# Two expert layers after attention: the first layer's expert groups become four blocks wide, and its late weight conversions are spread over the steps

## The chip, the cores and the metric

The kernel runs on one core of a Trainium2 chip. The metric is the device time in microseconds (us), median of several runs; before the change it is 1189.27 us. The core has TensorE (PE in the profile; PEld is its weight load), VectorE (DVE), ScalarE (ACT), GpSimd (POOL) and SyncE (SP), which here only issues DMAs.

## The reference

```python
scores = scale * q @ k.T                       # (4, 8, 576, 576)
scores = where(scores >= max(scores) - tau, scores, -1e9)
attn   = exp(scores - max); attn /= sum(attn) + 1e-9
x = (attn @ v), heads side by side             # (2304, 512)
# layer 1, w_in (512, 2048), w_out (2048, 512), both float64 in memory
h = x @ w_in;  g = h * sigmoid(1.702 * h);  x = g @ w_out
# layer 2, its own w_in and w_out
h = x @ w_in;  g = max(0.01 * h, h);        out = g @ w_out
```

## The kernel before

**Attention.** The 32 heads are worked off in 16 pairs (`p` = 0 to 15). Each pair's operations have one- or two-letter names with a number (`Q8` are scores, `E8` the exponent, `w8`, `h8`, `l8` a copy and the two halves of flipped probabilities, `V` the products with the values, `a`, `b`, `c` what follows), and the table `START` gives each a time. The program is written out in the order of these times; an engine works through its own instructions in that order. In the last pair's table stand also some operations of layer 1: `Xh`, `Xl` (split of x), `H0`, `H1` (hidden sums) and `G21`, `G11`, `G20` (loads of weights).

**Number format.** TensorE multiplies rounded values. Each operand is a high half (rounded) and a low half (the rest), and each product is three products. So x of a block of 512 tokens becomes `xh` and `xl` (`split_x`: ACT copies, then POOL or DVE subtracts), and a weight block `wih`, `wil` or `woh`, `wol`.

**Weights.** `stage` (part G) loads one block of 128 columns of `w_in` (n = 0) or 128 rows of `w_out` (n = 1) as float64 into one of three buffers (`w64`); the SP queue issues the loads in program order, and a load waits until its buffer has been read. `convert` turns it into the two halves in parts: A on ACT (into the work tile `wF`), B, C, D, K on DVE, H on ACT (high half), M on POOL (low half). K is the last reader of the load's buffer.

**Expert layers.** `d_ff` is cut into 16 blocks `f`. The tokens are five blocks `blk`, four of 512 and the last of 256. A step is one (`blk`, `f`): `hidden_sums` (12 matmuls into `h`), the activation (ACT into `gf`, DVE multiplies or takes the maximum), the halves `gh` (ACT) and `gl` (POOL), and, LA = 2 steps later, `product` (12 matmuls into the four tiles `y`). `GROUPS` says how many `f` form a group. The steps go through group after group, in each through the token blocks, in each through the group's `f`. After the last `f` of a group in a block, `collect` adds `y` to x (or copies it, in the first group), and only then can the next block's product write the four tiles.

**Order.** While a group runs, the weights of the next are converted (`plan` puts each part of each block of weights into a step). Layer 1 had groups of 2, 4, 4, 4, 2, so two of its groups have ten steps; there the plan is `fast`, all parts of a block of weights in one step, between the DVE multiply of that step and its `gh`. Elsewhere it is `slow`, A to M over four steps. Three blocks of weights (`CONVERTED`) are converted in the first pair, three more (`STAGED`) are loaded ahead. `splits` splits the next block's x while a block runs.

Of the kernel before, what the change touches and what calls it, by code (L numbers as in the profile page):

```python
# [8 lines left out]
F32 = mybir.dt.float32  # L9
F32R = mybir.dt.float32r  # L10
I32 = mybir.dt.int32
AF = mybir.ActivationFunctionType
# [3 lines left out]
P = 128  # L16
B, H, S, D = 4, 8, 576, 64
NTOK = B * S
DM, DFF = 512, 2048
NCB = DM // P  # L20
NF = DFF // P
HALF = S // 2
NPAIR = B * H // 2
# [1 line left out]
SB = 3  # L25
TB = 512

GROUPS = {1: (2, 4, 4, 4, 2), 2: (4, 4, 4, 4)}
LA = 2
GB = 4  # L30
CONVERTED = ((0, 0), (1, 0), (0, 1))
STAGED = ((1, 1), (2, 0), (2, 1))
WI, WO = 8, 7
HI_MAX = 15 * 2.0**13 - 2.0**-7

# [133 lines left out]
    },  # L169
# [26 lines left out]
def split(a, n):  # L196
    return a.rearrange("p (h x) -> p h x", h=n)
# [3 lines left out]
def attention_moe_moe(  # L201
# [12 lines left out]
    nc = tc.nc  # L214
# [6 lines left out]
    stg = ctx.enter_context(tc.tile_pool(name="stg", bufs=1))  # L221
# [11 lines left out]
    tau_b = cp.tile([P, 1], F32, name="tau_b")  # L233
    tau_p = cp.tile([P, 1], F32, name="tau_p")
    qs = cp.tile([P, 1], F32, name="qs")

    wslot, staged, floats = {}, {}, {}
# [3 lines left out]
    def wtiles(layer, f, n):  # L241

        size, na = (WI, WO)[n], NA[n]
        early = ((layer - 1) * NF + f) % size < na
        return [
            pools["a" if early else "b"].tile(
                [P, DM], F32R, tag="w" + "io"[n] + z, name=f"w{'io'[n]}{z}_{layer}_{f}", bufs=na if early else size - na
            )
            for z in "hl"
        ]  # L250
# [13 lines left out]
    def convert(layer, f, n, part):  # L264
        src = staged[layer, f, n]
        if wide:

            words = src.rearrange("p (n t) -> p n t", t=2)
            lo, hi = words[:, :, 0], words[:, :, 1]
            if part == "A":  # L270
                floats[layer, f, n] = stg.tile([P, DM], F32, tag="wF", name=f"wF{layer}_{f}_{n}", bufs=2)
            F = floats[layer, f, n]
            t = F.bitcast(I32)
            if part == "A":
                nc.scalar.activation(F, hi.bitcast(F32), AF.Abs)
            elif part == "B":
                nc.vector.tensor_scalar(out=F, in0=F, scalar1=2.0**-15, scalar2=HI_MAX, op0=ALU.max, op1=ALU.min)  # L277
            elif part == "C":
                nc.vector.tensor_scalar(  # L279
                    out=t, in0=t, scalar1=3, scalar2=0x3FFFFFFF, op0=ALU.logical_shift_left, op1=ALU.bitwise_and  # L280
                )
            elif part == "D":
                nc.vector.scalar_tensor_tensor(
                    out=t, in0=lo, scalar=29, in1=t, op0=ALU.logical_shift_right, op1=ALU.bitwise_or
                )
            elif part == "K":
                nc.vector.scalar_tensor_tensor(  # L287
                    out=t, in0=hi, scalar=-0x40000000, in1=t, op0=ALU.bitwise_and, op1=ALU.bitwise_or
                )
        else:  # L290
            F = src
        if part == "H":
            wslot[layer, f, n] = wtiles(layer, f, n)
            nc.scalar.copy(wslot[layer, f, n][0], F)
        elif part == "M":
            wh, wl = wslot[layer, f, n]
            nc.gpsimd.tensor_tensor(out=wl, in0=F, in1=wh, op=ALU.subtract)
# [5 lines left out]
    def span(blk):  # L303
        return slice(blk * TB, min(NTOK, (blk + 1) * TB))

    def split_x(layer, blk, c, on, part=None):

        cols = span(blk)
        w = cols.stop - cols.start
        hs, ls = xs_of.setdefault((layer, blk), ({}, {}))  # L310
        for n, z in (("h", hs), ("l", ls)):
            if part not in (None, n):
                continue
            z[c] = pools["x0" if blk == 0 else "x"].tile(
                [P, w], F32R, tag=f"x{n}{c}_{blk}", name=f"x{n}{layer}_{blk}_{c}", bufs=1
            )
        if part != "l":
            nc.scalar.copy(hs[c], x[c][:, cols])  # L318
        if part != "h":
            on.tensor_tensor(out=ls[c], in0=x[c][:, cols], in1=hs[c], op=ALU.subtract)  # L320
# [19 lines left out]
    with tc.tile_pool(name="at", bufs=1) as at, tc.manual_schedule():  # L340
        qm = []
        for i in range(2):
            t = at.tile([P, 384], F32R, name=f"qm{i}")
# [122 lines left out]
        def exponent(p, t):  # L466
            r = st[p]
            e = at.tile([P, S], F32, tag="e", name=f"e{p}_{t}", bufs=2)
            nc.scalar.activation(  # L469
                split(e, 2), r["s", t][:, :, 0:HALF], AF.Exp, bias=r["m"][:, t : t + 1], scale=-1.0  # L470
            )
            r["e", t] = e

        def threshold(p, t):
            c = slice(t, t + 1)
# [298 lines left out]
        for f in range(NA[0]):  # L774
            LAST[f"H{f}"] = (lambda p, z: hidden_sums(1, 0, z), (f,))
        for f, n in STAGED:
            LAST[f"G{f}{n}"] = (lambda p, *z: stage(*z), (1, f, n))
# [7 lines left out]
        todo = []  # L785
# [74 lines left out]
    def collect(layer, blk, gi):  # L860
# [3 lines left out]
        for e, y in enumerate(y_of.pop((layer, blk))):  # L864
# [8 lines left out]
            if gi == 0:  # L873
                (nc.vector.tensor_copy if e % 2 else nc.scalar.copy)(acc, y)
            elif layer == 1 or gi < len(GROUPS[2]) - 1:
                nc.vector.tensor_tensor(out=acc, in0=y, in1=acc, op=ALU.add)  # L876
# [21 lines left out]
    steps, first_step, order = [], [], []  # L898
    for l in (1, 2):
        f0 = 0  # L900
        for gi, size in enumerate(GROUPS[l]):
            first_step.append(len(steps))
# [6 lines left out]
    todo = {}  # L909

    def plan(item, s, parts):
        for part, d in parts.items():
            todo.setdefault(max(0, s + d), []).append(item + (part,))

    slow = dict(G=-4, A=0, B=1, C=1, D=2, K=2, H=3, M=3)
    fast = dict(G=-2, A=0, B=0, C=0, D=0, K=0, H=0, M=0)
    for i, item in enumerate(z for z in order[0] if z[1:] not in CONVERTED):
        plan(item, i, fast)
    for g, items in enumerate(order[1:]):
        room = (first_step + [len(steps)])[g + 1] - first_step[g]  # L920
        for i, item in enumerate(items):
            if room < 2 * len(items) + 3:
                plan(item, first_step[g] + 1 + i, fast)
            else:
                plan(item, first_step[g] + 3 + 2 * i, slow)

    def weight_parts(s, which):
        for l, f, n, part in todo.get(s, ()):
            if part in which:
                if part != "G":  # L930
                    convert(l, f, n, part)
                elif (l, f, n) not in staged:
                    stage(l, f, n)

    def splits(s):

        l, gi, size, blk, f, j = steps[s]
        nxt = s - j + size
        if nxt >= len(steps) or steps[nxt][1] or (steps[nxt][0], steps[nxt][3]) == (1, 1):
            return  # L940
        for c in range(j * NCB // size, (j + 1) * NCB // size):
            split_x(steps[nxt][0], steps[nxt][3], c, nc.vector if size < NCB and c % 2 else nc.gpsimd)

    for c in range(NCB):
        split_x(1, 1, c, nc.vector if c % 2 else nc.gpsimd)
    for s in range(len(steps) + LA):
        weight_parts(s, "G")
        if s < len(steps):
            l, gi, size, blk, f, j = steps[s]
            rest = hidden(l, blk, f)  # L950
            weight_parts(s, "ABCDKH")
            rest()
            weight_parts(s, "M")
            splits(s)
        if s >= LA:
            l, gi, size, blk, f, j = steps[s - LA]
            product(l, blk, f, j == 0, j == size - 1)
            if j == size - 1:
                collect(l, blk, gi)
# [28 lines left out]
```

## Time and profile before

| | us |
|---|---|
| median of 3 runs (1187.96 to 1189.45) | 1189.27 |
| the profiled execution, its own time | 1188.86 |
| its span in the profile | 1187.1 |
| PE busy in the span | 1133.6 |
| DVE busy | 663.6 |
| ACT busy | 586.3 |
| POOL busy | 586.3 |

Busy time of PE is modelled from overlapping matmuls; idle stretches and the clock granted to TensorE tell more. The attention fills the first 352 us, layer 1 the time to about 791, layer 2 the rest.

### The profile page before, as it was taken

What the parts mean: (1) busy time and instruction counts of PE and PEld (TensorE: products, weight loads), DVE (VectorE), ACT (ScalarE), POOL (GpSimd) and SP (SyncE); (2) the same over time, 40 slices, a digit from 0 to 9 for tenths busy, and PEclk for the clock granted to TensorE, in tenths of its full rate; (3) what the DMA queues carried; (4) which work ended last, traced back from release to release, by engine and by line L of the source; (5) the groups of instructions that cost most, each with busy time, mean ns of one, the idle gap of its engine ahead of it and who ended that gap; (6) DMA issues with size and microseconds to landing.
All of it is one profiled execution on the core that took longest, in us unless ns stands there. A gap on an engine that the chain in (4) does not pass through costs nothing.

```text
span 1187.1 us, 17037 instructions
## 1 busy us (share of the span) xinstructions
PE 1133.6 (95%) x6201; PEld 968.2 (82%) x6201; DVE 663.6 (56%) x1357; ACT 586.3 (49%) x1138; POOL 586.3 (49%) x519
## 2 busy tenths in 40 slices
PE   8998999999896799999999999889999999999997
PEld 7887898889884588888888888778888888888886
DVE  6999999999876633443452524843343352534232
ACT  6998989999884432332332322334433332332221
POOL 6787887877774423343343332455543333343221
PEclk8999999999997989999999999999999999999999
DMA  5332323221302201110110100211110110110022
GB/s 145 82 84 64 82 61 98 70 72 35 103 1 72 70 19 36 54 54 18 54 54 18 54 18 19 90 35 37 53 54 18 54 54 18 54 36 1 36 63 62
DMA packets 47619, 62.38 MB, mean 53 GB/s; under 512 B 10544, under 2 KB 39216, under 8 KB 47536
## 3 DMA queue, kind: packets, MB, share of 16 engines
q1 hardware_dynamic: 47536, 61.29, 18.3%
q8 instruction: 49, 0.80, 0.3%
q14 instruction: 34, 0.28, 0.1%
HBM read 47.71 MB, written 4.72 MB: 44 GB/s over the span
## 4 chain that ended last, share of the span: by engine, by line
PE 69%; DVE 14%; ACT 10%; issue 3%; POOL 2%; DMA 1%; SPq 0%; DVEq 0%; ACTq 0%; POOLq 0%
PE h L332 30%; PE y L858 17%; PE y L856 13%; ACT e L469 3%; PE pv L585 3%; DVE m L462 3%; DVE pp L490 2%; PE s L435 2%; PE pp L511 2%; ACT raw L533 1%; DVE wF L277 1%; DVE wF L279 1%; DVE wF L287 1%; DVE x L876 1%; ACT ptg1h L542 1%
## 5 line engine op out<-in xcount | busy, mean ns | idle before, releaser
L828 POOL TENSOR_TENSOR gl<-gf,gh 128x512 fp32r<-128x512 f32 (+1 forms) x160 | 205.6, 1285 | 511.2 <-ACT gh L827 476.7
L824 DVE TENSOR_TENSOR gf<-h,gf 128x512 f32<-128x512 f32 (+1 forms) x80 | 51.0, 638 | 239.8 <-ACT gf L823 239.8
L332 PE MATMUL h<-xh,wih 128*128 128x512 f32 (+1 forms) x640 | 160.6, 371 | 17.5 <-ACT xh L318 17.5
L821 DVE TENSOR_TENSOR gf<-h,gf 128x512 f32<-128x512 f32 (+1 forms) x80 | 50.9, 637 | 207.6 <-ACT gf L820 207.6
L332 PE MATMUL h<-xl,wih 128*128 128x512 f32 (+1 forms) x640 | 160.8, 372 | 2.5 <-POOL xl L320 2.3
L823 ACT ACTIVATE gf<-h 128x512 f32<-128x512 f32 (+1 forms) x80 | 44.5, 556 | 233.8 <-PE h L332 230.7
L332 PE MATMUL h<-xh,wil 128*128 128x512 f32 (+1 forms) x640 | 159.2, 371 | 0.0
L332 PEld LDWEIGHTS h<-xh,wih 128*128 128x128 f32 x640 | 114.8, 188 | 41.7 <-ACT xh L318 20.5
L820 ACT ACTIVATE gf<-h 128x512 f32<-128x512 f32 (+1 forms) x80 | 44.4, 555 | 201.8 <-PE h L332 201.7
L332 PEld LDWEIGHTS h<-xl,wih 128*128 128x128 f32 x640 | 114.9, 191 | 25.0 <-POOL xl L320 5.0
L332 PEld LDWEIGHTS h<-xh,wil 128*128 128x128 f32 x640 | 114.7, 190 | 20.4
L856 PE MATMUL y<-gh,woh 128*128 128x512 f32 (+1 forms) x320 | 119.6, 378 | 8.1 <-DVE x L876 5.5
L827 ACT CAST gh<-gf 128x512 fp32r<-128x512 f32 (+1 forms) x160 | 92.5, 578 | 59.6 <-DVE gf L824 33.6
L856 PE MATMUL y<-gh,wol 128*128 128x512 f32 (+1 forms) x320 | 118.4, 374 | 0.0
L469 ACT ACTIVATE e<-s,m 128x576 f32<-128x576 f32 x144 | 110.8, 772 | 11.4 <-DVE m L462 10.2
L462 DVE TENSOR_REDUCE m<-s 128x1 f32<-128x576 f32 x144 | 107.7, 751 | 13.1 <-PE s L435 8.4
L858 PE MATMUL y<-woh,gh 128*128 128x512 f32 x288 | 112.4, 390 | 0.0
L858 PE MATMUL y<-wol,gh 128*128 128x512 f32 x288 | 112.3, 390 | 0.0
L435 PE MATMUL s<-kt,qt 128*128 128x288 f32 x512 | 100.3, 318 | 10.2 <-DVE pp L490 5.4
L490 DVE SCALAR_TENSOR_TENSOR pp<-s,thr,e 128x576 f32<-128x576 f32 x128 | 103.4, 810 | 7.9 <-ACT e L469 6.6
L856 PE MATMUL y<-gl,woh 128*128 128x512 f32 (+1 forms) x320 | 91.7, 371 | 0.0
L435 PEld LDWEIGHTS s<-kt,qt 128*128 128x128 f32 x512 | 73.2, 191 | 21.5 <-DVE pp L490 12.3
(117 smaller groups left out, 2209.0 us busy)
## 6 DMA issues: line engine op xcount, KB each, us to landing
w<-in_moe_w_in_dram SPq DMA_DIRECT2D x32, 512.0 KB, 3.6
w<-in_moe_w_out_dram SPq DMA_DIRECT2D x32, 512.0 KB, 3.6
kt<-kt SPq DMA_DIRECT2D x30, 288.0 KB, 4.1
kn<-in_k_dram SPq DMA_DIRECT2D x16, 256.0 KB, 2.9
qn<-in_q_dram SPq DMA_DIRECT2D x16, 256.0 KB, 2.9
vn<-in_v_dram SPq DMA_DIRECT2D x16, 256.0 KB, 3.0
out_dram<-o SPq DMA_DIRECT2D x20, 128.0 KB, 2.4
out_dram<-o SPq DMA_DIRECT2D x8, 256.0 KB, 2.2
```

The source lines that it names most:

```text
L332: nc.tensor.matmul(h, lhsT=wt[:, c * P : (c + 1) * P], rhs=xx[c], start=i == 0 and c == 0, stop=i == 2 and c == NCB - 1)
L435: nc.tensor.matmul(sc[:, a, 0:HALF], lhsT=w, rhs=kt[n][:, c : c + HALF], start=n == 0, stop=n == 1)
L462: nc.vector.tensor_reduce(out=small(p, "m")[:, t : t + 1], in_=r["s", t][:, :, 0:HALF], axis=mybir.AxisListType.XY, op=ALU.min)
L469: nc.scalar.activation(split(e, 2), r["s", t][:, :, 0:HALF], AF.Exp, bias=r["m"][:, t : t + 1], scale=-1.0)
L490: nc.vector.scalar_tensor_tensor(out=split(dst, 2), in0=r.pop(("s", t))[:, :, 0:HALF], scalar=r["thr"][:, t : t + 1], in1=split(r.pop(("e" ...
L821: nc.vector.tensor_tensor(out=gf, in0=h, in1=gf, op=ALU.mult)
L823: nc.scalar.activation(gf, h, AF.Copy, scale=0.01)
L824: nc.vector.tensor_tensor(out=gf, in0=h, in1=gf, op=ALU.max)
L827: nc.scalar.copy(gh, gf)
L828: nc.gpsimd.tensor_tensor(out=gl, in0=gf, in1=gh, op=ALU.subtract)
L856: nc.tensor.matmul(ys[e][:, 0:w], lhsT=wt[:, at_e], rhs=g, start=first, stop=last)
L858: nc.tensor.matmul(ys[e], lhsT=g[:, at_e], rhs=wt, start=first, stop=last)
```

## The change

- Layer 1's groups become four of four blocks, like layer 2's.
- The first group's own late weights (five blocks of weights after the three converted ones) are sorted by the step that needs them and spread: A two steps ahead, B, C, D, K one step ahead, H and M in the step itself; some of it stands ahead of the first step (`weight_parts(-1, ...)`). The loads ahead are now (2,0), (3,0) and (1,1).
- The second group's weights follow in the slow pattern, two steps apart.
- Within every step H now follows `gh`, M follows `gl`, and A comes after the splits; before, A and H stood ahead of `gh`.
- `wF` has three buffers in place of two.
- The split of layer 1's second token block, which stood ahead of the first step, is done one chunk a step in the first four steps, all on POOL.
- After the last exponent (`E8` of pair 15) a one-element-wide sigmoid is put on ACT.

```diff
-GROUPS = {1: (2, 4, 4, 4, 2), 2: (4, 4, 4, 4)}
+GROUPS = {1: (4, 4, 4, 4), 2: (4, 4, 4, 4)}
-STAGED = ((1, 1), (2, 0), (2, 1))
+STAGED = ((2, 0), (3, 0), (1, 1))
...
-        "G21": 214030, ... "G11": 344475, ... "G20": 388894,
+        "G11": 214030, ... "G20": 344475, ... "G30": 388894,
...
-                floats[layer, f, n] = stg.tile([P, DM], F32, tag="wF", name=f"wF{layer}_{f}_{n}", bufs=2)
+                floats[layer, f, n] = stg.tile([P, DM], F32, tag="wF", name=f"wF{layer}_{f}_{n}", bufs=3)
...
+            if (p, t) == (NPAIR - 1, 8):
+
+                nc.scalar.activation(tau_b, tau_p, AF.Sigmoid)
...
-            todo.setdefault(max(0, s + d), []).append(item + (part,))
-
-    slow = dict(G=-4, A=0, B=1, C=1, D=2, K=2, H=3, M=3)
-    fast = dict(G=-2, A=0, B=0, C=0, D=0, K=0, H=0, M=0)
-    for i, item in enumerate(z for z in order[0] if z[1:] not in CONVERTED):
-        plan(item, i, fast)
+            todo.setdefault(max(-1, s + d), []).append(item + (part,))
+
+    late = [z for z in order[0] if z[1:] not in CONVERTED]
+    late.sort(key=lambda z: z[1] + (LA if z[2] else 0))
+    for i, item in enumerate(late):
+        plan(item, i, dict(G=-4, A=-2, B=-1, C=-1, D=-1, K=-1, H=0, M=0))
     for g, items in enumerate(order[1:]):
-        room = (first_step + [len(steps)])[g + 1] - first_step[g]
         for i, item in enumerate(items):
-            if room < 2 * len(items) + 3:
-                plan(item, first_step[g] + 1 + i, fast)
-            else:
-                plan(item, first_step[g] + 3 + 2 * i, slow)
+            plan(item, first_step[g] + len(late) * (g == 0) + 3 * (g > 0) + 2 * i, dict(G=-4, A=0, B=1, C=1, D=2, K=2, H=3, M=3))
...
-        if nxt >= len(steps) or steps[nxt][1] or (steps[nxt][0], steps[nxt][3]) == (1, 1):
+        if nxt >= len(steps) or steps[nxt][1]:
...
-    for c in range(NCB):
-        split_x(1, 1, c, nc.vector if c % 2 else nc.gpsimd)
+    weight_parts(-1, "GABCDK")
     for s in range(len(steps) + LA):
         weight_parts(s, "G")
         if s < len(steps):
             l, gi, size, blk, f, j = steps[s]
             rest = hidden(l, blk, f)
-            weight_parts(s, "ABCDKH")
+            weight_parts(s, "BCDK")
             rest()
-            weight_parts(s, "M")
+            weight_parts(s, "HM")
             splits(s)
+            weight_parts(s, "A")
```

## Rows read from the trace of the kernel before

**Rows 1.** The page's 40 slices: granted clock of TensorE, in tenths.

```profile
PEclk8999999999997989999999999999999999999999
```

**Rows 2.** Stretches of the expert layers: busy time of each engine, granted clock, DMA.

```profile
352.04:426.78 74.74, 54.44 (x208) 41.88 (x205) 44.86 (x63) 33.02 (x63) 35.31 (x27) 0.84 0.21 64
728.65:794.26 65.61, 59.19 (x278) 47.22 (x277) 46.03 (x69) 24.36 (x45) 29.66 (x24) 1.00 0.21 65
```

**Rows 3.** The chain that ended last, in order of time: start, us, what.

```profile
417.97 4.79 PE y L856 x12
...
440.75 2.72 PE h L332 x12
...
511.46 1.43 PE h L332 x12
...
519.82 2.41 DVE x L876 x4
...
522.27 1.21 PE y L856 x8
```

**Rows 4.** TensorE in order of time; idle before an instruction in brackets.

```profile
352.04 1.20 PE L332 MATMUL h<-xh,wih 128*128 128x512 f32 x4
...
360.42 0.50 PE L856 MATMUL y<-gh,woh 128*128 128x512 f32 x1 [2.65 <-ACT gh L827]
```

**Rows 5.** Two stretches after idle TensorE, columns as in Rows 2.

```profile
379.74:384.50 4.76, 4.76 (x10) 3.28 (x11) 2.02 (x3) 1.44 (x3) 3.71 (x3) 0.50 0.21 77
384.90:393.00 8.10, 8.10 (x37) 6.70 (x36) 5.16 (x9) 4.32 (x8) 3.36 (x3) 1.00 0.21 65
```

**Rows 6.** TensorE in the second stretch of Rows 2.

```profile
771.82 0.47 PE L856 MATMUL y<-gh,woh 128*128 128x512 f32 x1 [1.86 <-DVE x L876]
```

**Rows 7.** ScalarE in order of time, end of the attention and first step.

```profile
344.42 0.74 ACT L469 ACTIVATE e<-s,m 128x576 f32<-128x576 f32 x1 [0.79 <-DVE m L462]
...
347.27 0.43 ACT L570 CAST rtg1h<-pr 128x320 fp32r<-128x320 f32 x1 [0.61 <-PE pr L556]
348.12 0.59 ACT L533 COPY raw<-pp 128x512 f32<-128x512 f32 x1 [0.43 <-PE pp L511]
...
350.20 0.21 ACT L619 ACTIVATE inv<-sum 128x5 f32<-128x5 f32 x1
...
352.10 2.18 ACT L318 CAST xh<-x 128x512 fp32r<-128x512 f32 x4
354.31 1.28 ACT L820 ACT_TABLE_LOAD   x1
```

**Rows 8.** Groups of instructions from 352 to 427 us, shapes apart: count, busy us, mean ns.

```profile
L828 POOL TENSOR_TENSOR gl<-gf,gh 128x512 fp32r<-128x512 f32 x8 | 10.3, 1287 | 31.7 <-ACT gh L827 31.7
...
L275 ACT ACTIVATE wF<-w 128x512 f32<-128x512 f32 x9 | 6.0, 662 | 0.0
...
L827 ACT CAST gh<-gf 128x512 fp32r<-128x512 f32 x8 | 4.9, 613 | 0.0
L820 ACT ACTIVATE gf<-h 128x512 f32<-128x512 f32 x8 | 4.8, 594 | 7.1 <-PE h L332 7.0
```

**Rows 9.** VectorE in order of time.

```profile
352.71 0.49 DVE L656 TENSOR_TENSOR x<-pn,xs 128x320 f32<-128x320 f32 x1
...
357.32 0.43 DVE L279 TENSOR_SCALAR wF<-wF 128x512 int32<-128x512 int32 x1
357.78 0.69 DVE L283 SCALAR_TENSOR_TENSOR wF<-w,wF 128x512 int32<-128x512 int32 x1
...
362.05 1.39 DVE L279 TENSOR_SCALAR wF<-wF 128x512 int32<-128x512 int32 x1
```

**Rows 10.** GpSimd in order of time.

```profile
361.69 1.46 POOL L297 TENSOR_TENSOR wol<-wF,woh 128x512 fp32r<-128x512 f32 x1
```

**Rows 11.** Loads of the weight buffers between 340 and 427 us.

```profile
DMA to landing us min/median/max: 3.5/3.6/3.8
```

**Rows 12.** TensorE in layer 2's first group.

```profile
870.18 0.39 PE L332 MATMUL h<-xl,wih 128*128 128x256 f32 x1 [0.60 <-POOL xl L320]
```

6 rows, old and new, of the table START are left out of this document.

## The prediction

> **What bounds the kernel now.** I read the 40 slices first: TensorE's granted clock is full but for three places, one of them around 355 to 425 us, where the attention hands over to layer 1 [rows 1]. The chain in order of time says what sets the end there: in steady state nothing but matmuls, 12 in 2.72 us for a full block and in 1.43 us for the half block [rows 3]. So a group of steps has a floor that can be counted, and a stretch's loss is its length less its matmuls.
>
> First group before, from H0's first matmul to the first hidden sum of group 2, 74.74 us [rows 2, 4]: 7 full and 2 half hidden sums and 8 full products, 15 x 2.72 + 2 x 1.43 = 43.7 us. Loss 31.1 us, at a granted clock of 0.84.
>
> Last group of layer 1 and the change to layer 2, 65.61 us [rows 2]: 10 full and 2 half hidden sums, 8 full and 3 half products, 18 x 2.72 + 5 x 1.43 = 56.1 us. Loss 9.5 us. One of its waits is 1.86 us of TensorE for an addition on VectorE, which stood behind four conversions in its queue [rows 6].
>
> These are the two groups of ten steps, planned `fast`. The groups of twenty lose little: at such a group's end the full product ends when VectorE's additions begin, 519.82; one half hidden sum (1.43) is all TensorE has before the next half product, whose last 8 matmuls begin at 522.27, behind those additions, and end at 523.48 [rows 3]. Without a wait that product would have ended at 519.82 + 2 x 1.43 = 522.68: 0.8 us an end.
>
> **The change part by part.** The matmuls stay the same. Three places change, and I walk each.
>
> *End of the attention.* The early sigmoid puts a table load of 1.28 us [rows 7] and a small activation (0.21, as the one of 128x5) behind E8, which ends at 345.16. ScalarE then has slack: 0.61 us before `rtg1h` and 0.43 before the last copy `raw` [rows 7]. So 1.5 - 1.04 = 0.5 to 0.6 us reach the attention's end. I take +0.6; below, 0, if more slack hides it; above, 1.5. The load that is removed (354.31) was no gain here: H0's matmuls, begun at 352.04, end only at about 354.8, so the first activation waits for them about as long [rows 4, 7]. The Trainium skill (ScalarE: Activation LUTs, What ACT_TABLE_LOAD costs) counts another 1.38 us of drain with each switch; the trace shows none, for the load begins where the casts before it end, 352.10 + 2.18 = 354.28 against 354.31 [rows 7]. By the page the sum below would be 1.4 us longer.
>
> *First group.* Five late blocks of weights are converted while the first steps run. What decides is how VectorE and GpSimd get along. Part C takes 0.43 us alone, but 1.39 when GpSimd runs beside it: it starts at 362.05, M ends at 361.69 + 1.46 = 363.15, C at 363.44 [rows 9, 10]. So one of the two waits for the other, and each gets in behind the other's current instruction. The parts cost, alone, B and C 0.45 each, D and K 0.72 with the gap [rows 9]; `gl` 1.29 [rows 8], and M and `xl`, of the same shape, as much. ScalarE: A 0.66, cast 0.61, `gf` 0.59 [rows 8]; the multiply as D, 0.7. In a step of the new plan stand B, C, D, K (2.3) and `gl`, M, `xl` (3.8): 6 us one after another, against 5.44 of matmuls. The walk, alternating, all 0.6 us later than before:
>
> - Ahead of the steps: VectorE is free at 353.20 + 0.6 = 353.8 [rows 9]; conversion of (2,0) to 356.1. H0 352.6 to 355.4.
> - Step 0: multiply to 356.8, `gh` 357.4, H of (2,0) 358.0. Then B, C of (1,1), `gl`, D, M of (2,0) (360.8), K (361.4), `xl` (362.7). Step 2's hidden sum starts at 358.0 and must wait at its fifth matmul for M; at 360.8 it goes on, at half clock 8 x 0.43, to 364.2. Product 0 to 366.9.
> - Step 1: the multiply waits for K, 361.4 to 362.1; `gh`, H, `xh` to 363.8. The load of (2,1) waited for K of (1,1) too: issued 361.5, landed 3.6 later [rows 11], 365.1. A of (2,1) stands in ScalarE's queue ahead of step 2's `gf`, which so starts at 365.8. VectorE and GpSimd alternate to K of (3,0), 368.2.
> - Step 2: multiply to 368.9, H of (3,0) 370.1, M 372.9. Hidden sum 3: four matmuls from 370.1 at half clock, the rest from 372.9 to 375.6. Product 1 to 378.3.
> - Step 3: `gf` 376.2, multiply 376.9, H of (2,1) 378.1, `gl` 379.0, M 380.9, last `xl` of block 1 382.8. Hidden sum 4 waits for it, to 383.0; product 2 385.7, hidden sum 5 388.5 (M of (3,1) is done by then, 387.5), product 3 391.2.
>
> From here TensorE has two steps' lead. Since 352.04 it has done 5 hidden sums and 4 products, 9 x 2.72 = 24.5 us, in 39.2: a loss of 14.7 us, the 0.6 included. Gain 31.1 - 14.7 = 16.4 us.
>
> The half clock: after 2.65 idle us [rows 4] and more, TensorE ran at a granted clock of 0.50, that is 1.2 of 2.4 GHz, for 4.8 us, then at 1.00 [rows 5]; 12 matmuls took 4.79 us in place of 2.72 [rows 3]. I have it twice in the walk; a third time, at product 2, would be +1.5.
>
> *Rest of group 1.* In the steps that follow the three engines fit into 5.44 us (GpSimd 2.6, every second step 3.9; VectorE 0.7 + 0.9 or 1.4). The chunk split in a block's last step is needed by the next hidden sum; layer 2's first group, built the same, lost 0.60 us by it [rows 12]: +0.6. The second group's conversions end two steps into it, ahead of their use. One more end of a twenty-step group (0 to 1): +0.8.
>
> *Layer 1 to layer 2.* The ten-step group goes; its place takes an end like the one above (0.8), with layer 2's first split in its four half steps: `gl` 0.7 (an estimate, a little over half of the full one's 1.29), `xl` 1.29, M 1.29 in two of four, conversions 0.9 or 1.4, some 15.2 us against 14.0 of matmuls. The last `xl` comes about 0.7 to 1.2 us late. Loss 2.0 in place of 9.5: gain 7.5; at best 8.7, at worst 4.
>
> A, H, M behind `gh`, `gl` in all other steps, and the third `wF` buffer: nothing; TensorE's work of two steps (10.9 us) hides them. Without that cover each would cost its 0.6.
>
> **Sum**, against the profiled execution: 1188.86 + 0.6 + 0.8 - 16.4 - 7.5 = 1166.4. The median shown is 0.4 above that execution, so **1167**.
>
> **The rivals.**
>
> *The engines do not block each other so much* (the lock rule is wrong in size, or `gl` and M fall between the conversions). The same walk with every instruction at its time alone ends the four products at 385.3, loss 8.8; with the best transition: 31.1 - 8.8 + 8.7 - 0.8 - 0.6 = 29.6 saved, 1159. For it: D and K at 0.69 in many places. Against: C at 1.39 [rows 9]. Chance 0.18.
>
> *The queue of ScalarE holds the group back.* (2,1) and (3,1) are not loaded ahead; the A that waits for the load stands ahead of the next `gf`, and that of everything else in the step; the clock falls a third time. Two late loads of some 2 us each beyond the walk, 1.5 of clock, and the transition at its worst: loss 20 and 5.5, saved 31.1 - 20 + 9.5 - 5.5 - 1.4 = 13.7, 1175. Chance 0.15.
>
> *Slower than before.* The walk has short waits in every one of the first steps. If these keep TensorE at the lower level on through the group, a full step costs 2 x 4.79 = 9.6 in place of 5.44 us; 22.5 / 4.2 = 5.4 such steps beyond the walk eat the gain, ten of them give 1209. Against it: once matmuls followed each other, the clock was back after 4.8 us [rows 5]. Chance 0.03.
>
> *The plan does not spread:* an in-order queue makes the first steps as serial as before, and only the last group's gain is left, within some us of 1181; chance 0.02. And 0.02 within 0.2%, which is about what a measurement of this kernel tells from no change.
>
> The Trainium skill (SBUF — State Buffer, SBUF: two separate sides) has a rule that speaks against putting this work side by side: VectorE in its two-port forms or with two SBUF inputs, and GpSimd, take one port pair by an exclusive lock, for a whole instruction. Rows 9 and 10 agree ([rows 9, 10]: C ends 0.29 us after M). By it the walk's 1167 holds, without it the first rival's 1159.
>
> **How the numbers follow.** Forecast 0.60, with its own range 1163 to 1171. The 8-in-10 range takes in the first rival's end and the second's: 1159 to 1175. Faster: 0.60 + 0.18 + 0.15 + 0.02 = 0.95; same 0.02; slower 0.03.
>
> **What would show it.** The sigmoid's table load behind E8 and H0 about 0.6 us later. B, C, D, K of (2,0) before the first multiply, about 353.8 to 356.1; C or D at some 1.3 us beside GpSimd in steps 0 to 3. Product 3 ends at about 391; from then on 5.44 us a step to the end of the block, no idle TensorE above 1 us before the group's end. Between layer 1 and 2 at most two waits, of about 1 us. The prediction is wrong if product 3 ends before 387 or after 396, if ScalarE waits for a load in every step, or if the transition still loses more than 5 us.

## The result, and the profile after

| | before | after | |
|---|---|---|---|
| median, us | 1188.77 (1187.96 to 1189.45, 4 runs) | 1169.22 (1168.12 to 1170.26, 4 runs) | ratio 0.9838, 95% interval 0.9823 to 0.9854 |
| profiled execution, its own time | 1188.86 | 1169.74 | 19.1 less |
| its span | 1187.1 | 1168.0 | 19.1 less |

One run of an experiment below, 1246.24 us at a granted clock of 0.845 where all others have 0.98 or more, is left out of its median. The forecast was 1167, its own range 1163 to 1171.

The 40 slices first, as in [rows 1]. Before, the granted clock was below 9 in the first slice, in the 13th (356 to 386 us, a 7) and in the 15th (415 to 445 us, an 8); the last two, which the prediction put down as one place, begin in the first group, and the change to layer 2 had no dip. After the change the 15th slice is at 9 and the 13th at 8.

```profile
PEclk8999999999998999999999999999999999999999
```

Then the stretches. The first row is the first group from H0's first matmul to the end of product 3; the next three are pieces of it; the last is the change from layer 1 to layer 2 (columns as in [rows 2]).

```profile
356.26:394.70 38.44, 30.00 (x113) 22.80 (x110) 22.98 (x24) 14.64 (x28) 22.56 (x16) 0.87 0.18 55
364.40:367.60 3.20, 3.20 (x8) 2.58 (x9) 3.17 (x4) 2.09 (x4) 3.01 (x3) 0.55 0.43 128
375.50:380.80 5.30, 5.29 (x13) 4.13 (x14) 1.28 (x3) 0.65 (x2) 1.64 (x1) 0.50 0.32 99
386.60:400.00 13.40, 13.40 (x61) 11.07 (x60) 4.13 (x7) 7.10 (x13) 6.61 (x6) 1.00 0.11 35
748.34:775.08 26.74, 25.98 (x157) 22.70 (x157) 12.29 (x23) 10.88 (x22) 19.04 (x16) 1.00 0.19 59
```

In the 38.44 us stand 5 hidden sums and 4 products, 24.5 us at the full rate: a loss of 14.0 us, where the walk had 14.1 behind H0. It has two stretches at half clock (0.55 and 0.50), as many as the walk counted, the second one four matmuls later than there; from 386.6 on TensorE is full. The change of layers holds 5 x 2.72 + 8 x 1.43 = 25.0 us of matmuls, so it loses 1.7 us (forecast 2.0; 9.5 before).

TensorE's waits in order of time, which answer to [rows 4, 6, 12]:

```profile
361.86 1.20 PE L332 MATMUL h<-xh,wih 128*128 128x512 f32 x4 [2.58 <-ACT wih L294]
364.38 2.08 PE L332 MATMUL h<-xh,wil 128*128 128x512 f32 x4 [1.32 <-POOL wil L297]
373.00 1.21 PE L332 MATMUL h<-xh,wih 128*128 128x512 f32 x4 [2.43 <-ACT wih L294]
375.51 2.07 PE L332 MATMUL h<-xh,wil 128*128 128x512 f32 x4 [1.30 <-POOL wil L297]
386.17 0.50 PE L332 MATMUL h<-xl,wih 128*128 128x512 f32 x1 [0.81 <-POOL xl L320]
451.78 0.39 PE L332 MATMUL h<-xl,wih 128*128 128x256 f32 x1 [0.60 <-POOL xl L320]
...
560.19 0.39 PE L859 MATMUL y<-gh,woh 128*128 128x256 f32 x1 [0.40 <-DVE x L879]
...
766.22 0.50 PE L332 MATMUL h<-xl,wih 128*128 128x512 f32 x1 [0.37 <-POOL xl L320]
```

The reader sees the walk here: hidden sum 2 waits for its high half, four matmuls later for its low half, and hidden sum 3 does the same. Counted from H0's first matmul, the walk had hidden sum 2 at 5.4 and 8.2 us (measured 5.6 and 8.1), hidden sum 3 at 17.5 and 20.3 (16.7 and 19.3), the last `xl` at 30.4 (29.9).

But H0 itself came at 356.26, in place of 352.04 [rows 4]: 4.2 us later, where the forecast had 0.6. The chain that ended last shows why (start, us, what):

```profile
318.11 6.14 DMA w<-in_moe_w_in_dram
324.27 0.69 ACT wF L275
324.98 0.44 DVE wF L277
325.44 0.44 DVE wF L279
325.90 0.69 DVE wF L283
...
328.00 0.60 DVE wF L287
...
348.57 1.28 ACT L475
349.86 0.20 ACT tau_b L475
```

Parts A to K of (2,0) run at 324 to 329 us, in the middle of the last pair of the attention, and not behind it at 353.8 as the walk had them. They need nothing of the attention, and they are written ahead of the steps; the built program has them before the last pair's own waiting work. So for these six instructions it does not hold that an engine works in the order in which the program is written out; what in the build moves them was not found out. ScalarE's row there waits for the load:

```profile
324.27 1.24 ACT L275 ACTIVATE wF<-w 128x512 f32<-128x512 f32 x2 [2.01 <-DMA w<-in_moe_w_in_dram]
...
348.57 1.28 ACT L475 ACT_TABLE_LOAD   x1
349.86 0.20 ACT L475 ACTIVATE tau_b<-tau_p 128x1 f32<-128x1 f32 x1
...
359.31 0.60 ACT L823 ACTIVATE gf<-h 128x512 f32<-128x512 f32 x1 [3.01 <-PE h L332]
...
362.23 0.66 ACT L275 ACTIVATE wF<-w 128x512 f32<-128x512 f32 x1
```

The 4.2 us split into three, by the first scores of the last pair behind its key exchange (321.20 before, 321.89 after), H1 (343.72, 347.11) and H0 (352.04, 356.26): 0.7 ahead of that pair, 22.52 to 25.22 = 2.7 in it, 8.32 to 9.15 = 0.8 from H1 to H0, where the early table load stands. The 0.7 need not be the change's: in the profiles of the changed kernel and of the edits below that lie behind that place, these first scores come anywhere from 320.02 to 322.75.

VectorE in the first steps, which answers to [rows 9]:

```profile
361.46 1.74 DVE L283 SCALAR_TENSOR_TENSOR wF<-w,wF 128x512 int32<-128x512 int32 x1
363.24 1.63 DVE L287 SCALAR_TENSOR_TENSOR wF<-w,wF 128x512 int32<-128x512 int32 x1
364.80 0.68 DVE L824 TENSOR_TENSOR gf<-h,gf 128x512 f32<-128x512 f32 x1
365.40 0.90 DVE L277 TENSOR_SCALAR wF<-wF 128x512 f32<-128x512 f32 x1
366.33 1.44 DVE L279 TENSOR_SCALAR wF<-wF 128x512 int32<-128x512 int32 x1
367.81 1.66 DVE L283 SCALAR_TENSOR_TENSOR wF<-w,wF 128x512 int32<-128x512 int32 x1
```

And GpSimd beside it, which answers to [rows 10]:

```profile
362.62 1.71 POOL L297 TENSOR_TENSOR wil<-wF,wih 128x512 fp32r<-128x512 f32 x1
364.29 1.73 POOL L320 TENSOR_TENSOR xl<-x,xh 128x512 fp32r<-128x512 f32 x1
366.20 1.28 POOL L831 TENSOR_TENSOR gl<-gf,gh 128x512 fp32r<-128x512 f32 x1 [0.19 <-ACT gh L830]
367.45 1.47 POOL L297 TENSOR_TENSOR wol<-wF,woh 128x512 fp32r<-128x512 f32 x1
```

Ends lie one behind the other: M to 364.33, K to 364.87, `xl` to 366.02, C to 367.77, M to 368.92, D to 369.47. Each engine gets in once between two instructions of the other, and D, 0.69 alone [rows 9], takes 1.66 and 1.74 here.

### The profile page after: what moved, and what is told of

It is laid out like the page before. It is cut to its first block, busy times and chain, and to the rows that moved or that the text cites. A ratio compares the mean times of both kernels' runs of the same rounds, so it can differ in the third digit from the quotient of the medians.

```text
span 1168.0 us, 16925 instructions
## 1 busy us (share of the span) xinstructions
PE 1129.2 (97%) x6201; PEld 968.5 (83%) x6201; DVE 639.3 (55%) x1327; ACT 589.1 (50%) x1139; POOL 602.6 (52%) x529
## 4 chain that ended last, share of the span: by engine, by line
PE 74%; DVE 10%; ACT 9%; issue 4%; POOL 2%; DMA 1%; DVEq 0%; ACTq 0%; SPq 0%; POOLq 0%
PE h L332 32%; PE y L861 17%; PE y L859 15%; ACT e L469 3%; DVE m L462 3%; PE pv L588 3%; DVE pp L493 2%; PE s L435 2%; PE pp L514 2%; ACT raw L536 1%; ACT ptg1h L545 1%; ACT kt L405 1%; ACT qt L413 1%; ACT sh L603 1%; POOL xl L320 1%
## 5 line engine op out<-in xcount | busy, mean ns | idle before, releaser
L831 POOL TENSOR_TENSOR gl<-gf,gh 128x512 fp32r<-128x512 f32 (+1 forms) x160 | 210.6, 1316 | 473.1 <-ACT gh L830 452.4
L332 PE MATMUL h<-xh,wih 128*128 128x512 f32 (+1 forms) x640 | 158.1, 369 | 5.0 <-ACT wih L294 5.0
L859 PE MATMUL y<-gl,woh 128*128 128x512 f32 (+1 forms) x320 | 88.5, 368 | 0.0
```

What stands on the lines that cost most here:

```text
L332: nc.tensor.matmul(h, lhsT=wt[:, c * P : (c + 1) * P], rhs=xx[c], start=i == 0 and c == 0, stop=i == 2 and c == NCB - 1)
L831: nc.gpsimd.tensor_tensor(out=gl, in0=gf, in1=gh, op=ALU.subtract)
L859: nc.tensor.matmul(ys[e][:, 0:w], lhsT=wt[:, at_e], rhs=g, start=first, stop=last)
```

## The experiments

Each kernel is the changed one with the edit shown; every ratio is to the kernel before, run beside it. "First group" is H0's first matmul to the end of product 3 (38.44 us in the changed kernel's profile), "last pair" the first scores behind the key exchange to H1 (25.22; 22.52 before). Behind product 3 all the changed kernels take the same time, 773.1 to 773.6 us to the end of the span, so what an edit is worth lies ahead of it. How often the clock falls in the first group differs from profile to profile (see the repeat at the end), which is worth 1.7 us there.

**The loads earlier.** The loads of (2,0) and (3,0) get earlier times in the last pair's table.

```diff
-        ... "G20": 344475, ... "G30": 388894, ...
+        ... "G20": 235000, "G30": 256000, ...
```

> The changed kernel with one edit: the three loads ahead, (1,1), (2,0), (3,0), are all issued before pair 14 instead of (2,0) and (3,0) in pair 15. Theory: the attention's end came 3.4 us later than before because ScalarE stood 2.0 us in pair 15, waiting for the load of (2,0) that the first conversion needs. Then the conversion finds its data, no such wait shows, H0 starts at about 353.5 to 354.5 instead of 356.3, and the time is 1.5 to 3 us below the changed kernel's 1169.2: 1166 to 1167.7. Rival: it is the conversion work itself (1.2 us of ScalarE, 2.2 us of VectorE) among the attention's instructions; then H0 starts where it did, within 0.7 us, and the time is that of the changed kernel within 0.7 us.

Measured: 1167.38 us (1166.69 to 1170.43), ratio 0.9827, 0.9808 to 0.9846. The last pair is back at 22.55 us, but the conversions moved with their load into the twelfth pair, and that pair went from some 16.1 to 19.08 us in the profiled execution (1170.43, the slowest of the four). ScalarE waits for no load there. H0 came at 357.06, 0.8 later than in the changed kernel, and not at 353.5 to 354.5. So in this profile work put into a pair costs about 3 us there as well; the other three runs (1166.7 to 1168.0) lie in the range of the theory and leave open whether it always does.

**The sigmoid table late.** The early one-element sigmoid is left out.

```diff
-            if (p, t) == (NPAIR - 1, 8):
-                nc.scalar.activation(tau_b, tau_p, AF.Sigmoid)
```

> The changed kernel without the small sigmoid behind the last exponent, so that the table is loaded ahead of the first activation of layer 1. Theory: ScalarE is idle for 3.0 us there, so the load of 1.28 us is hidden, and the attention's last copies come 0.8 us earlier: H0 at about 355.4 and the time 0.6 to 1.0 us below the changed kernel's. Rival: the load lies on the path at its new place; then the first activation comes up to 1.3 us later behind H0 and the time is the same or up to 0.5 us longer.

Measured: 1169.24 us (1168.95 to 1169.7), ratio 0.9838, 0.9823 to 0.9853. ScalarE in order of time:

```profile
355.63 1.28 ACT L820 ACT_TABLE_LOAD   x1
358.63 0.60 ACT L820 ACTIVATE gf<-h 128x512 f32<-128x512 f32 x1 [1.71 <-PE h L332]
```

The load is over at 356.91, and the activation still waits 1.71 us for H0's matmuls: it comes 3.06 us behind H0's first matmul (355.57) here and 3.05 in the changed kernel. From H1 to H0 it is 8.30 us in place of 9.15. So the early table costs 0.8 us at the attention's end and buys nothing; the expected gain of 0.6 to 1.0 us in the median did not show, and the medians do not resolve it.

**The old plan in the new groups.** The late weights have all parts in one step, and A and H stand ahead of `gh` again.

```diff
-        plan(item, i, dict(G=-4, A=-2, B=-1, C=-1, D=-1, K=-1, H=0, M=0))
+        plan(item, i, dict(G=-4, A=0, B=0, C=0, D=0, K=0, H=0, M=0))
...
-            weight_parts(s, "BCDK")
+            weight_parts(s, "ABCDKH")
             rest()
-            weight_parts(s, "HM")
+            weight_parts(s, "M")
             splits(s)
-            weight_parts(s, "A")
```

> The changed kernel with the late weights' conversions not spread: all parts A to H of one block of weights in one step, between the multiply and the high half of g, one block a step in steps 0 to 4, and A and H in that place in all later steps too; groups of four, sorted order, loads and table as in the changed kernel. Theory: most of the gain comes from the groups (the ten-step groups are gone), and the spreading is worth only the share of the first four steps: each step is a chain of A, B, C, D, K, H, cast, subtracts and a hidden sum, some 8 to 9 us, so product 3 ends 4 to 9 us later than in the changed kernel, less up to 3 us that the attention gains because no conversion stands in it: 1171 to 1176. Rival: the spreading brings most of it; then the time is above 1180.

Measured: 1175.43 us (1173.09 to 1175.85), ratio 0.9886, 0.987 to 0.9902. The first group, in the view of stretches:

```profile
353.56:400.94 47.38, 31.66 (x113) 23.06 (x109) 19.87 (x29) 16.78 (x31) 20.56 (x17) 0.86 0.18 56
```

The first group takes 8.9 us longer, the last pair 2.7 less, since nothing is converted ahead of the steps (22.52 us). The groups, with the rest of the change, bring 13.3 of the 19.5 us, the spreading 6.2. The A of (2,0) needs a load alone here too, but it is written behind the first activation, and it ran there, at 357.11: what it depends on and where it is written both count.

**The halves a step earlier.** H and M of a late block of weights stand in the step of its K.

```diff
-        plan(item, i, dict(G=-4, A=-2, B=-1, C=-1, D=-1, K=-1, H=0, M=0))
+        plan(item, i, dict(G=-4, A=-2, B=-1, C=-1, D=-1, K=-1, H=-1, M=-1))
...
-    weight_parts(-1, "GABCDK")
+    weight_parts(-1, "GABCDKHM")
```

> The changed kernel with H and M of each late block one step earlier, in the step of its B, C, D, K, still behind the halves of g; for (2,0) ahead of the first step. Theory: TensorE's three long waits in the first group are for the high and low half of (2,0) and (3,0), which stand behind the g halves of the step that needs them; a step earlier, hidden sum 2 follows H0 with under 1 us of idle time and hidden sum 3 waits under 2 us, product 3 ends 4 to 8 us earlier against H0's start, and the time is 1161 to 1166. Rival: the shared work of VectorE and GpSimd (some 6 us a step) sets the pace whatever the order; then the first four steps take as long as before and the time is within 1.5 us of the changed kernel's.

Measured: 1171.59 us (1171.06 to 1174.37), ratio 0.9865, 0.9844 to 0.9885. My theory fell, and the rival, within 1.5 us, does not fit either. ScalarE in order of time:

```profile
363.64 0.62 ACT L294 CAST woh<-wF 128x512 fp32r<-128x512 f32 x1 [2.73 <-DVE wF L287]
...
370.00 0.62 ACT L294 CAST wih<-wF 128x512 fp32r<-128x512 f32 x1 [2.74 <-DVE wF L287]
```

H now waits 2.7 us for the K of its own step, and `xh`, A and the next `gf` stand behind it in ScalarE's queue; so the next multiply and the next K come later too, one step every 6.4 us. TensorE then waited 6.34 us at hidden sum 3 and 5.31 at hidden sum 4, for a cast of `xh`; the first group took 40.28 us.

**The conversions behind the attention.** What stood ahead of the steps gets the last times of the last pair's table, so that it runs where the walk had put it.

```diff
+        "A20": 476000, "A11": 476001, "B20": 476002, "C20": 476003, "D20": 476004, "K20": 476005,
...
+        for part, f, n in (("A", 2, 0), ("A", 1, 1), ("B", 2, 0), ("C", 2, 0), ("D", 2, 0), ("K", 2, 0)):
+            LAST[f"{part}{f}{n}"] = (lambda p, *z: convert(*z), (1, f, n, part))
...
-    weight_parts(-1, "GABCDK")
+    weight_parts(-1, "G")
```

> The changed kernel, with the conversions that stand ahead of the first step (A, B, C, D, K of (2,0) and A of (1,1)) put behind the attention's last operations on ScalarE and VectorE, so that none runs inside pair 15. Theory: the 3.4 us by which the attention ended late came from these few instructions standing in pair 15 (the load waited for, or their work); behind the attention both engines are idle for 2.5 to 3.0 us before the first activation, room enough for 1.2 and 2.3 us. Then H0 starts 2.5 to 3.4 us earlier, the first group takes as long from H0 on, within 1 us, and the time is 1165.5 to 1167. Rival: the attention's end moved for another reason (run by run, or the loads' places); then H0 starts where it did in the changed kernel, and the conversions behind it make the time the same or up to 2 us longer.

Measured: 1166.07 us (1164.75 to 1166.93), ratio 0.981, 0.9796 to 0.9823. The conversions run from 354.03 to 356.36, the walk's own place; they cost nothing there, since H0's matmuls run beside them: hidden sum 2 starts 5.60 us behind H0 as in the changed kernel. The last pair is 22.50 us, 2.7 less than in the changed kernel:

```profile
321.31:343.81 22.50, 22.10 (x169) 20.25 (x170) 20.36 (x53) 19.68 (x40) 18.83 (x19) 1.00 0.15 48
```

**One engine's work taken away.** The second token block's low halves are not computed; the products that need them multiply `xh` in their place, so the output is not the reference's.

```diff
...
+            if (layer, blk) == (1, 1):
+                ls[c] = hs[c]
+            else:
-            on.tensor_tensor(out=ls[c], in0=x[c][:, cols], in1=hs[c], op=ALU.subtract)
+                on.tensor_tensor(out=ls[c], in0=x[c][:, cols], in1=hs[c], op=ALU.subtract)
```

> The changed kernel, with the low half of x left out for layer 1's second token block: its high half is multiplied in its place, so four GpSimd subtractions in steps 0 to 3 are gone and the matmuls are the same in number. Theory: VectorE's conversion parts and GpSimd's subtractions exclude one another, each getting in behind the other's current instruction; then just those parts that had stood beside the left-out subtraction fall to their time alone: B of (3,0) from 0.90 to about 0.42, K of (3,0) from 1.67 to about 0.69, K of (1,1) and of (2,1) still long beside M, and product 3 ends 2 to 4 us earlier against H0's start. Rival: parts C, D and K are long for their own sake (float64 words read with a stride, buffers being loaded); then their durations in steps 0 to 3 stay within 0.1 us.

Measured: 1165.71 us (1163.26 to 1165.94), ratio 0.9803, 0.979 to 0.9817. The first group takes 33.45 us: 5.0 less, but 3.3 less than the repeat below, which like this run has one fall of the clock and not two. VectorE in step 1:

```profile
366.69 0.41 DVE L277 TENSOR_SCALAR wF<-wF 128x512 f32<-128x512 f32 x1
367.14 0.43 DVE L279 TENSOR_SCALAR wF<-wF 128x512 int32<-128x512 int32 x1
367.60 1.73 DVE L283 SCALAR_TENSOR_TENSOR wF<-w,wF 128x512 int32<-128x512 int32 x1
369.36 1.67 DVE L287 SCALAR_TENSOR_TENSOR wF<-w,wF 128x512 int32<-128x512 int32 x1
```

B fell from 0.90 to 0.41 us, where `xl` had stood beside it, and C from 1.44 to 0.43, since it was now all but done when `gl` began; D and K did not fall, since `gl` and M stood beside them. So K of (3,0), which the theory had at 0.69, stayed at 1.67. The 16 conversion parts of steps 0 to 3 took 16.96 us in place of 18.35, and all of that is step 1 (5.67 to 4.24); in the others, where `gl` and M stand beside D and K in both kernels, they took 4.2 to 4.3 as before. The edit also takes away the wait for `xl`, so it does not part the two effects.

**The weights' halves first.** In the first five steps H and M stand ahead of `gh` and `gl`.

```diff
             weight_parts(s, "BCDK")
+            if s < len(late):
+                weight_parts(s, "HM")
             rest()
-            weight_parts(s, "HM")
+            if s >= len(late):
+                weight_parts(s, "HM")
```

> The changed kernel, with H and M of the late blocks of weights ahead of the halves of g in the first five steps (same steps, other order within the step). Theory: hidden sums 2 and 3 wait for H and M because these stand behind the cast and the subtraction of the step's g halves, which are wanted only two steps later; ahead of them, H of (2,0) follows the first activation at once, hidden sum 2 starts 1 to 1.5 us earlier and its fifth matmul 2 to 2.5, hidden sum 3 the same, product 3 ends 2 to 4.5 us earlier against H0's start; time 1165 to 1167.5. Rival: the conversions' pace on VectorE (6.3 us from multiply 1 to multiply 2) sets hidden sum 3 and all after it; then at most 1 us is saved, 1168 to 1169.5.

Measured: 1166.51 us (1164.98 to 1166.7), ratio 0.9812, 0.9798 to 0.9825. TensorE's waits:

```profile
359.18 1.20 PE L332 MATMUL h<-xh,wih 128*128 128x512 f32 x4 [1.19 <-ACT wih L294]
360.88 1.19 PE L332 MATMUL h<-xh,wil 128*128 128x512 f32 x4 [0.50 <-POOL wil L297]
...
370.90 2.07 PE L332 MATMUL h<-xh,wih 128*128 128x512 f32 x4 [5.20 <-ACT wih L294]
```

Hidden sum 2 waits 1.69 us in place of 3.90; one long wait is left at hidden sum 3, 5.20 in place of 2.43 and 1.30, and the first group takes 35.43 us with one fall of the clock: 3.0 less than the changed kernel's profile, 1.3 less than the repeat. All five runs lie below all eight of the changed kernel (1168.12 and more), so the place that the change gave to H and M is the worse one in these five steps; how much of the gain is the clock's stays open.

**The three together**: conversions behind the attention, no early sigmoid, halves first.

> The changed kernel with three edits joined: the first conversions behind the attention's last operations, H and M ahead of the halves of g in the first five steps, and no early sigmoid. Theory: the three gains add, 2.7 + 3 + 0.8, the time is 1161.5 to 1164. Rival: they overlap, because the table load and the conversions of (2,0) then share the 3 us before the first activation; 1165 to 1167.

Measured: 1161.83 us (1161.57 to 1162.55), ratio 0.9776, 0.9763 to 0.9789. H0 starts at 351.13, the first group takes 35.45 us:

```profile
351.13:386.58 35.45, 28.36 (x113) 21.87 (x109) 27.32 (x28) 17.23 (x31) 21.87 (x16) 0.90 0.24 75
```

It beats both kernels. The sum of the parts, 3.2 + 2.7 + at most 0.8 = 6.7 us, is near the 7.4 measured. By stretches, against the changed kernel's profile: 2.7 in the last pair, 0.85 from H1 to H0, and 3.0 in the first group, with one fall of the clock in place of two.

**What costs in the last pair: the wait or the work.** The conversions stay in the last pair, at places behind the landing of their load; beside it ran the changed kernel once more.

```diff
+        "A20": 350436, "A11": 350437, "B20": 353590, "C20": 355790, "D20": 357180, "K20": 360185,
...
```

> The first step's conversions stay in the last pair of the attention, but behind the landing of the load of (2,0), at chosen places of that pair's order, so that no engine waits for a load there. Theory (the work itself): 2.2 us of VectorE and 2.5 us of ScalarE work put anywhere into this pair lengthen it by 1.5 to 3 us, so from the first scores after the swap of kt to H1 it takes 24 to 25.5 us, and the time is 1168 to 1169.5 us, like the changed kernel. Rival (the wait for the load): without a wait the pair stays at 22.5 to 23.3 us, and the time is 1166 to 1167 us, as with the conversions behind the attention.

> The changed kernel once more, beside the run above and in the same call. Both theories: 1168 to 1170.5 us, the last pair 25 to 25.5 us, H0's first matmul between 355.5 and 357 us.

Measured: 1169.27 us (median of 5 runs, 1167.38 to 1170.57), ratio 0.9838, 0.9825 to 0.9851; the changed kernel 1169.78 (1168.42 to 1170.23), ratio 0.984, 0.9828 to 0.9853. ScalarE converts without a wait, and the last pair is longer still. ScalarE in order of time:

```profile
331.97 1.27 ACT L276 ACTIVATE wF<-w 128x512 f32<-128x512 f32 x2
```

The pair itself, in the view of stretches, then the same pair in the changed kernel and in its repeat:

```profile
321.90:348.43 26.53, 24.04 (x169) 21.46 (x170) 23.62 (x57) 20.96 (x42) 19.75 (x19) 0.94 0.19 61
321.89:347.11 25.22, 21.98 (x170) 20.32 (x170) 22.32 (x57) 20.88 (x42) 19.01 (x19) 1.00 0.21 64
322.64:348.68 26.04, 22.19 (x169) 20.33 (x170) 23.85 (x57) 20.99 (x42) 19.30 (x19) 1.00 0.20 62
```

So the work alone is enough, and the rival's forecast (22.5 to 23.3 us without a wait) falls. VectorE is busy 20.36 us of the 22.50 without conversions and 23.62 of 26.53 with them: 3.3 us more of VectorE, 4.0 more of the pair. Part of the 4.0 is the clock: it was granted 0.94 in this pair and 1.00 without conversions, and TensorE's own busy time grew by 1.9 us. B, C, D, K take 3.33 us here and not 2.2, since K took 1.60 in this pair too. The changed kernel's two profiles, both at 1.00, fit: 25.22 and 26.04 us for a VectorE busy 22.32 and 23.85, and the longer one has the shorter wait for the load (1.3 us against 2.0). Not shown is that the wait costs nothing in the changed kernel, where the load stands in the chain; nor was ScalarE's share, 1.3 us more work, parted from VectorE's.

The repeat shows also what one profile is worth. Its H0 came at 357.82, its first group took 36.77 us:

```profile
357.82:394.59 36.77, 28.79 (x113) 21.82 (x109) 22.98 (x24) 14.65 (x28) 22.57 (x16) 0.91 0.19 58
365.95:371.20 5.25, 5.25 (x12) 4.13 (x13) 5.15 (x6) 2.84 (x5) 5.07 (x4) 0.50 0.33 101
374.50:386.00 11.50, 8.62 (x35) 6.34 (x35) 7.89 (x7) 3.35 (x6) 8.86 (x6) 1.00 0.26 81
```

Here the granted clock stayed at half through the last eight matmuls of hidden sum 2 and into product 0, and did not fall again at hidden sum 3. The waits up to there come at the same distances from H0 in both profiles (hidden sum 3 at 16.7 and 19.2 us). The same code, once with two falls and once with one: 1.7 us. It was made up by an H0 1.6 us later, so both profiles' product 3 ends at 394.6 or 394.7.

## Why the prediction was right, and where it was wrong

Forecast 1167 and measured 1169.2, by the mechanism that it named, but with two errors.

- *Attention's end, +0.6 predicted, +4.2 measured: the step that failed.* The sentence "VectorE is free at 353.20 + 0.6 = 353.8 [rows 9]; conversion of (2,0) to 356.1" took it that what is written ahead of the steps runs behind the attention. It ran in the last pair and cost 2.7 us. The run with the conversions behind the attention puts them where the walk had them: 3.2 us faster. That the conversions' work makes the pair longer without any wait for a load was shown by placing it behind the landing. The order in the written program was not enough to know the place; the walk should have asked which of the moved instructions depend on a load alone. Of the rest of the 4.2, 0.7 lies ahead of that pair and varies from profile to profile.
- *The early table, +0.6 predicted, +0.8 measured* (8.30 against 9.15 from H1 to H0). Right in size and in "no gain". The page of the Trainium skill weighed there (ScalarE: Activation LUTs, What ACT_TABLE_LOAD costs) counts a drain besides; in the profile after, the load begins 0.02 us after the exponent's end (347.81 + 0.74 = 348.55) and the sigmoid 0.01 after the load's: none here either.
- *First group, loss 14.1 behind H0 predicted, 14.0 measured* (12.3 in the repeat, with one fall of the clock in place of two). The two waits of hidden sums 2 and 3 and that of the last `xl` came within about 1 us of their places, which is the mechanism; that the loss agrees to 0.1 us is in part luck, since the same kernel lost 1.7 less in its repeat. Within it two steps were wrong, in opposite directions: the load of (2,1) was to be issued at 361.5 and to hold ScalarE; it was issued at 328.66, because K of (2,0) had freed its buffer in the last pair, and no A waited. Step 2's `gf` so started 11.6 us behind H0, not 13.2. Against that, D and K took 1.63 to 1.75 us in each of steps 0 to 3, more often than the walk had them.
- *The engines block each other.* Right. The first rival needed D and K at 0.69 beside GpSimd; they took 1.63 to 1.75. The Trainium skill (SBUF — State Buffer, SBUF: two separate sides) says that GpSimd and VectorE, in its two-port forms or with two SBUF inputs, share a port pair under an exclusive lock held for an instruction; the ends one behind the other agree with it.
- *The queue of ScalarE* did not hold the changed kernel back, but that rival is real: the run with the halves a step earlier is it, by another door, and cost 2.4 us.
- *The plan does not spread* was refuted by the old plan in the new groups: 6.2 us slower.
- *Rest of group 1*: 0.60 for the split, measured 0.60; an end of a group 0.8, measured 0.8 (the half hidden sum and half product at 557.59 take 3.66 us, not 2.86; one wait of 0.40 shows, at 560.19).
- *A, H, M behind `gh`, `gl` in all other steps: nothing.* Right for A and H: with these ahead of `gh` again in all steps, the old plan took 773.2 us behind product 3, the changed kernel 773.3.
- *Layer 1 to layer 2*: loss 2.0 predicted, 1.7 measured.
- *The sum*: 22.5 predicted, 19.1 measured against the profiled execution. Attention's end accounts for 3.6 of it the wrong way, the first group and the change of layers for 0.1 and 0.3 the other way; 0.2 stays open.

Left open: what in the build moves the conversions, and whether the conversions cost as much in the twelfth pair as in the last, since one profile says 3 us and three of the four times say less.

## What to carry to other kernels

Before costing work that is "put ahead" of a stage, look at what it depends on: if only a load, it may run inside the stage before. There it cost 2.7, 3.5 and 4.0 us in three profiles, in a pair whose VectorE was already busy 20.4 of 22.5 us; behind that pair it cost nothing. Where the next matmuls wait for a weight's halves and the lead of TensorE is still short, the halves go ahead of the activation's halves in the queues; once it had two steps of lead, the order of A and H made no difference (773.2 and 773.3 us). And an instruction moved a step ahead must not land in a queue before the result that it reads: it then delays everything behind it.

## What the runs showed of the hardware

- VectorE and GpSimd side by side took turns by instruction in these rows; a conversion of 0.43 to 0.69 us then takes 1.4 to 1.7. Removing 6.4 us of GpSimd's work (four `xl`) gave VectorE back only 1.4 us, and all of that in step 1: in the other three steps `gl` and M, not `xl`, stood beside the long D and K.
- The same program has one or two stretches at half clock (1.2 of 2.4 GHz). Behind the same waits of hidden sum 2 (2.58 and 1.32 us) TensorE ran at 0.55 for 3.20 us in one profile and at 0.50 for 5.25 in the other; at hidden sum 3, a wait of 2.43 us and another of 1.30 came with a fall to 0.50 in the first, waits of 1.18 and 1.31 in the repeat with none.
- A table load of ScalarE began 0.02 us behind the exponent before it, and the next activation 0.01 us behind the load: 1.28 us and no drain beside it. Where the engine would have waited for matmuls anyway, the load cost nothing.
